# Loads of v and of three weight slices issued from GpSimd's queue, in a fused attention and SwiGLU kernel

## The chip, the core and the metric

The kernel runs on one core of a Trainium2 chip. The metric is the device time of one execution in microseconds. Times of several runs are given as a median; one execution more was taken with the hardware profiler, and all rows below come from that one.

The names in the rows: PE is TensorE's matmul, PEld its weight load, DVE is VectorE, ACT is ScalarE, POOL is GpSimd and SP is SyncE, which does no arithmetic and here issues DMA transfers. SPq and ACTq are the instructions of an engine's sequencer, DMA issues above all.

## What is computed

```python
def _attn_ref(q, k, v):                       # 4 batches, 12 heads, 448 rows, 64 columns
    scores = np.matmul(q, k.transpose(0, 1, 3, 2)) / np.sqrt(64) - np.log(448)
    attn = 1.0 / (1.0 + np.exp(-scores))
    return np.matmul(attn, v)

def _moe_ref(x, w_gate, w_val, w_out, rms_g): # x is 1792 x 768, the inner width is 1536
    rms = np.sqrt(np.mean(x * x, axis=-1, keepdims=True) + 1e-06)
    xn = x / rms * rms_g
    g = xn @ w_gate
    return g * (1.0 / (1.0 + np.exp(-g))) * (xn @ w_val) @ w_out
```

All inputs and the output are float32. The attention's weights are a sigmoid, so no row sum is needed.

## The kernel before

**Stages.** The attention goes over 24 pairs of heads (4 batches by 6). Then the SwiGLU products go over 12 slices (`fc`) of the inner width, and at the end the output products are made. The middle and the last stage begin after the attention's last pair, but the first three weight slices that the middle stage needs are loaded and prepared while the attention runs.

**One pair of the attention.** `load_qk` brings q and k of the pair, 224 KB each. On DVE `qk_hi` (L200) and `qk_lo` (L204) split them into two float16 parts in `nat_b`. `transpose` (L207) is a DMA that turns both round into `t_b`, of which there are three, so a pair's buffer is free when the pair three before it has been used by its scores. `k_swap` (L214, L215) makes two more copies of k on DVE. `scores` (L232) has 28 matmuls in four groups; ACT makes the sigmoid of each group (L234). `av` (L245) multiplies by v in 8 float32 matmuls, which the trace lists as 16. `load_v` (L195) brings v of a pair in two transfers of 128 KB into one of three buffers `v_b`.

**Order.** The order is written out by hand. The loop takes two groups of scores and then the `av` of the two groups before. Behind the four groups of pair `i` stand, in `FILL`: the transpose of pair `i + 2`; `k_swap(i + 1)` and `load_qk(i + 5)`; `qk_hi(i + 3)` and `load_v(i + 2)`; and `qk_lo(i + 3)`. Each engine and each queue works through its own list in order, and an instruction that waits for a semaphore holds everything behind it.

**Weights.** `load_w(fc, kind)` puts three transfers of 256 KB into the list `loads`; `run_load` takes one off the list after each half pair. They land in the two buffers `raw_w` (gate and val), one of each. `split_w` turns the words round on DVE (`to_f32`, L349, L352 and L353) and makes sums and float16 parts of them (L395, L398, L401). The loads of the next slice may overwrite `raw_w` only after L353 has read the buffer. The pieces of `split_w` and of the row norm (`norm`, with L275, L296 and L302) stand in the list `later`, from which the loop of the attention takes some in each step.

**SP's queue.** Before the change all loads and the DMA transposes stand in SP's one list, in program order:

```python
nc.sync.dma_start(dst, src[:, :, MID * n * D : (MID * n + 4) * D])      # v, L195
nc.sync.dma_start_transpose(out=..., in_=nat_b[i % 2]...)               # L207
nc.sync.dma_start(dst, src.rearrange("(c p) f -> p c f", p=P))          # weights, L364
```

Of the kernel before, what the change touches and what calls it, by code (L numbers as in the profile page):

```python
# [24 lines left out]
def attention_then_swiglu(  # L25
# [21 lines left out]
    nc = tc.nc  # L47
    B, H, S, D = q.shape
    DFF, DM = w_out.shape
    P = 128  # L50
    NPAIR = H // 2
    NSLOT = 2 * S // P
    MID = S // P
# [135 lines left out]
    def load_v(i):  # L189
        b, hp = pairs[i]  # L190
        t = v_b[i % 3].rearrange("p (j n) d -> p j n d", j=2)
        src = v[b, 2 * hp : 2 * hp + 2].rearrange("j (r c) d -> r j (c d)", c=NSLOT)
        for n in range(2):
            dst = t[64 * n : 64 * n + 64, :, 1 - n : 5 - n].rearrange("p j n d -> p j (n d)")
            nc.sync.dma_start(dst, src[:, :, MID * n * D : (MID * n + 4) * D])  # L195

# [159 lines left out]
    def load_w(fc, kind):  # L358


        def part(c):
            src = (w_gate, w_val)[kind][c * P : (c + 2) * P, 2 * fc * P : 2 * fc * P + 2 * P]
            dst = raw_w[kind][:, c : c + 2].rearrange("p c f w -> p c (f w)")
            nc.sync.dma_start(dst, src.rearrange("(c p) f -> p c f", p=P))  # L364

        loads.extend((fc, lambda c=c: part(c)) for c in range(0, NCC, 2))

# [307 lines left out]
    def ahead_by(n, part):  # L675
# [3 lines left out]
        (ahead_by(2, transpose),),  # L679
        (ahead_by(1, k_swap), ahead_by(5, load_qk)),  # L680
        (ahead_by(3, qk_hi), ahead_by(2, load_v)),
        (ahead_by(3, qk_lo),),
    )
# [7 lines left out]
    with tc.manual_schedule():  # L691
# [9 lines left out]
        transpose(0)  # L701
        load_qk(2)
        load_v(0)
        for part in (qk_hi, qk_lo, transpose, load_v, ahead_by(2, load_qk)):
            part(1)
# [147 lines left out]
```

## Time and profile before

| what | value |
|---|---|
| median of 3 runs | 619.05 us (617.21 to 619.07) |
| the profiled execution | 621.39 us, its span 619.6 us |
| PE busy | 599.4 us, 97% of the span |
| DVE busy | 484.4 us, 78% |
| ACT busy | 260.1 us, 42% |
| POOL busy | 1.1 us, 9 instructions |
| DMA | 62.73 MB in 84219 packets, nearly all on one queue |

Busy shares are means over stages with different limits. The attention reaches from the start to about 178 us, the SwiGLU products from there to 463 us, the output products from there to the end. A view by windows gives busy times, the granted TensorE clock (a share of 2.4 GHz: 1.00 is 2.4 and 0.50 is 1.2 GHz), the mean share of time in which the 16 DMA engines have a packet under way, and what they move.

### The profile page before, as it was taken

To read this page: it belongs to the slowest core of one execution; us is meant where nothing else is said; L and a number is where in the kernel's file an instruction comes from. 1 tells how busy PE (TensorE), PEld (TensorE's weight loads), DVE (VectorE), ACT (ScalarE), POOL (GpSimd) and SP (SyncE) were. 2 spreads that over 40 slices of the span, in tenths; PEclk is the share of its full clock that TensorE was granted. 3 is DMA by queue.
4 is the path that set the end of the run, shared out by engine and by line. 5 is a ranking of instruction groups with operands and counts; after the bars stand their busy time and mean duration, and the time that the engine had idled before them with its cause. 6 is when DMAs were issued, how large, how long until landed. Compare 5 with 4: busy or idle time off the path is not lost.

```text
span 619.6 us, 9157 instructions
## 1 busy us (share of the span) xinstructions
PE 599.4 (97%) x3594; PEld 322.9 (52%) x3594; DVE 484.4 (78%) x752; ACT 260.1 (42%) x392; POOL 1.1 (0%) x9
## 2 busy tenths in 40 slices
PE   8987999799999999999999999999999999999997
PEld 6433455364445555555555555555556666656664
DVE  4549799699879678878878878888889997776651
ACT  3666688497754423233143243243232244221020
POOL 0000000000000000000000000000000000000000
PEclk9998999799999999999999999999999999999999
DMA  7999979967500003303203113123147005121112
GB/s 176 234 242 232 251 173 228 238 157 175 142 0 2 2 0 103 100 3 103 79 24 103 53 50 103 40 63 103 58 138 314 0 7 119 30 51 26 33 46 51
DMA packets 84219, 62.73 MB, mean 101 GB/s; under 512 B 48336, under 2 KB 82640, under 8 KB 84176
## 3 DMA queue, kind: packets, MB, share of 16 engines
q1 hardware_dynamic: 83856, 61.76, 38.4%
q8 instruction: 28, 0.46, 0.3%
q10 hardware_dynamic: 320, 0.39, 0.2%
q14 instruction: 15, 0.12, 0.1%
HBM read 45.62 MB, written 5.51 MB: 83 GB/s over the span
## 4 chain that ended last, share of the span: by engine, by line
PE 84%; DMA 6%; DVE 4%; ACT 3%; issue 2%; SPq 1%; DVEq 0%; ACTq 0%
PE cc L425 13%; PE cd L425 13%; PE ca L425 13%; PE o L514 11%; PE cb L425 7%; PE av L245 6%; PE sc L232 6%; PE oc L601 4%; PE od L601 4%; PE oa L601 4%; DMA xc<-xc 4%; PE ob L601 2%; DMA xc<-in_k_dram 1%; ACT room L234 1%; PE rinv L302 1%
## 5 line engine op out<-in xcount | busy, mean ns | idle before, releaser
L425 PEld LDWEIGHTS <-wr 128*128 128x128 f16 x1512 | 147.9, 98 | 138.7 <-issue 1.2
L234 ACT ACTIVATE room<-sc,bias_s 128x896 f32<-128x896 f32 x96 | 83.9, 932 | 37.2 <-PE sc L232 37.0
L425 PE MATMUL ca<-xc,wr 128*128 128x448 f16 x432 | 89.6, 352 | 0.0
L232 PE MATMUL sc<-xc 128*64 128x448 f16 x672 | 75.9, 358 | 10.5 <-DVE xc L215 6.4
L245 PE MATMUL av<-room 128*64 128x448 f32 x384 | 84.4, 557 | 0.1
L232 PEld LDWEIGHTS <-xc 128*64 128x64 f16 x672 | 41.8, 111 | 53.6 <-issue 21.6
L425 PE MATMUL cc<-xc,wr 128*128 128x448 f16 x324 | 67.2, 352 | 0.0
L425 PE MATMUL cd<-xc,wr 128*128 128x448 f16 x324 | 67.2, 352 | 0.0
L514 PE MATMUL o<-xc,room 128*128 128x384 f16 x354 | 58.3, 326 | 0.0
L453 ACT ACTIVATE room<-ca 128x448 f32<-128x448 f32 x24 | 13.0, 543 | 90.3 <-PE ca L425 90.3
L514 PEld LDWEIGHTS <-room 128*128 128x128 f16 x354 | 34.6, 98 | 22.9
L245 PEld LDWEIGHTS av<-room 128*64 128x64 f32 x384 | 29.2, 140 | 30.1 <-issue 24.4
L425 PE MATMUL cb<-xc,wr 128*128 128x448 f16 x216 | 44.8, 352 | 0.0
L401 DVE SCALAR_TENSOR_TENSOR wr<-wr 128x768 f16<-128x768 f32 (+1 forms) x48 | 39.0, 851 | 0.1
L480 ACT ACTIVATE room<-room 128x448 f32<-128x448 f32 x24 | 13.8, 576 | 53.0 <-DVE room L479 53.0
L398 ACT ACTIVATE wr<-wr 128x768 f16<-128x768 f32 (+1 forms) x48 | 34.1, 753 | 3.5 <-DVE wr L395 3.5
L448 DVE TENSOR_TENSOR room<-room,cb 128x448 f32<-128x448 f32 x24 | 14.9, 621 | 19.6 <-PE cb L425 19.4
L353 DVE SCALAR_TENSOR_TENSOR wr<-wr 128x768 uint32<-128x768 uint32 x28 | 26.8, 957 | 0.9
L352 DVE SCALAR_TENSOR_TENSOR wr<-wr 128x768 uint32<-128x768 uint32 x28 | 26.8, 956 | 0.5
L204 DVE SCALAR_TENSOR_TENSOR xc<-xc 128x896 f16<-128x896 f32 (+1 forms) x25 | 26.3, 1051 | 0.5
L441 ACT ACTIVATE room<-ca 128x448 f32<-128x448 f32 x24 | 13.0, 544 | 32.0 <-PE ca L425 27.6
L395 DVE TENSOR_TENSOR wr<-wr 128x384 f32<-128x384 f32 x48 | 25.8, 553 | 0.8
(138 smaller groups left out, 709.4 us busy)
## 6 DMA issues: line engine op xcount, KB each, us to landing
wr<-in_moe_w_gate_dram SPq DMA_DIRECT2D x36, 256.0 KB, 3.3
wr<-in_moe_w_val_dram SPq DMA_DIRECT2D x36, 256.0 KB, 3.7
room<-in_v_dram SPq DMA_DIRECT2D x48, 128.0 KB, 3.7
xc<-in_q_dram SPq DMA_DIRECT2D x24, 224.0 KB, 3.4
xc<-in_k_dram SPq DMA_DIRECT2D x24, 224.0 KB, 3.2
out_dram<-room SPq DMA_DIRECT2D x49, 96.0 KB, 2.2
wr<-in_moe_w_out_dram SPq DMA_DIRECT2D x6, 768.0 KB, 4.3
xc<-in_moe_w_out_dram SPq DMA_DIRECT2D x5, 768.0 KB, 6.4
```

The lines of the kernel that those rows point to most:

```text
L204: stt(n[:, :, :, 1], ld_b[i % 4][:, t], SQ, n[:, :, :, 0], ALU.mult, ALU.subtract)
L232: nc.tensor.matmul(o, m, r, start=(w == 0), stop=(w == 1))
L234: nc.scalar.activation(a[:, :n], ps[:, :n, :S], AF.Sigmoid, bias=bias_s, scale=1.0 / (math.sqrt(D) * SQ * SQ))
L245: nc.tensor.matmul(ps[64 * j : 64 * j + 64, :S], v_b[i % 3][:, NG + j if g == MID else 1 + 5 * j + g], a[:, 0 if g == MID else j], start=( ...
L352: lambda: stt(b, r[:, :, 0], 29, b, ALU.logical_shift_right, ALU.bitwise_or),
L353: lambda: stt(b, r[:, :, 1], 0xC0000000, b, ALU.bitwise_and, ALU.bitwise_or),
L395: first.append((lambda o=o, f0=f0, f1=f1: tt(wf[:, o], wf[:, f0], wf[:, f1], ALU.subtract), 0.6))
L398: nc.scalar.activation(t[:, 0, s], wf[:, s], AF.Copy, scale=SW)
L401: stt(t[:, 1, s], wf[:, s], SW, t[:, 0, s], ALU.mult, ALU.subtract)
L425: nc.tensor.matmul(ps, w[:, l, b, c], xc[n, a][:, r, c], start=(not more and c == 0 and m == 0), stop=(c == NK - 1 and m == 2), skip_group ...
L514: nc.tensor.matmul(ps[:, :HALF], h[c, t // NTOK][:, l, t % NTOK * P : t % NTOK * P + P], wo[c][:, r, e * HALF : e * HALF + HALF], start=(c ...
L601: nc.tensor.matmul(ps[:, :HALF], a[x](m, l), b[y](m, r), start=(not more and m == 0 and n == 0), stop=(m == NFC // 2 - 1 and n == 2), skip ...
```

## The change

Two transfers get another issuing engine. Nothing else is changed: the same bytes go to the same places, and the program's order is the same.

```diff
@@ load_v
-            nc.sync.dma_start(dst, src[:, :, MID * n * D : (MID * n + 4) * D])
+            nc.gpsimd.dma_start(dst, src[:, :, MID * n * D : (MID * n + 4) * D])
@@ load_w, part
-            nc.sync.dma_start(dst, src.rearrange("(c p) f -> p c f", p=P))
+            queue = nc.gpsimd if fc < 3 else nc.sync
+            queue.dma_start(dst, src.rearrange("(c p) f -> p c f", p=P))
```

All 48 transfers of v and the 18 of weight slices 0 to 2 leave SP's list; slice 3 and all later ones stay. What stands behind the added line has a number higher by one (L364 is now L365).

At the start of SP's list, where the first three transposes (L207) stand between the loads of q and k (L186, L187), the difference is this:

```order
 L186 DMA xc<-in_q_dram 128x448
 L187 DMA xc<-in_k_dram 128x448
-L195 DMA room<-in_v_dram 64x2x256 x2
 L207 DMA_TRANSPOSE xc<-xc 128x14x128
-L195 DMA room<-in_v_dram 64x2x256 x2
 L186 DMA xc<-in_q_dram 128x448
 L187 DMA xc<-in_k_dram 128x448
 L186 DMA xc<-in_q_dram 128x448
 L187 DMA xc<-in_k_dram 128x448
```

The second transpose now follows the load of k directly, and the third has four transfers fewer ahead of it.

Where the loads of weight slice 2 begin, SP's list had these rows before, with the semaphores that each waits for (DVE and PE are the engines' own, DMAHW those of earlier transfers):

```order
L207 DMA_TRANSPOSE xc<-xc 128x14x128 [waits DMAHW7_49,DVE_49,PE_49]
L186 DMA xc<-in_q_dram 128x448 [waits DMAHW0_49]
L187 DMA xc<-in_k_dram 128x448 [waits DMAHW1_49]
L195 DMA room<-in_v_dram 64x2x256 [waits DMAHW2_49,PE_49]
L195 DMA room<-in_v_dram 64x2x256 [waits DMAHW3_49,PE_49]
L364 DMA wr<-in_moe_w_gate_dram 128x2x256 [waits DMAHW4_49,DVE_49]
L207 DMA_TRANSPOSE xc<-xc 128x14x128 [waits DMAHW5_49,PE_49]
```

The same transfers of v and of the weights stand in POOL's list now (DMASW are the semaphores of its own earlier transfers):

```order
L195 DMA room<-in_v_dram 64x2x256 [waits DMASW6_49,PE_49]
L195 DMA room<-in_v_dram 64x2x256 [waits DMASW7_49,DMASW5_49,PE_49]
L365 DMA wr<-in_moe_w_gate_dram 128x2x256 [waits DVE_49]
L365 DMA wr<-in_moe_w_gate_dram 128x2x256
L195 DMA room<-in_v_dram 64x2x256 [waits DMASW0_49,PE_49]
L195 DMA room<-in_v_dram 64x2x256 [waits DMASW1_49,PE_49]
```

The weight load that waits for DVE now holds the loads of v behind it, and on SP there is no such wait ahead of that transpose any more.

The start of POOL's list, behind its own memsets, is this:

```order
L195 DMA room<-in_v_dram 64x2x256 [waits Pool_49]
masks.py:199 ISA
masks.py:199 AFFINE_SELECT ident<-ident 128x128 [waits Pool_49]
L195 DMA room<-in_v_dram 64x2x256 x5
L365 DMA wr<-in_moe_w_gate_dram 128x2x256
L195 DMA room<-in_v_dram 64x2x256 [waits DMASW0_49,PE_49]
```

The v of the first three pairs and the first weights, which stood behind loads and transposes on SP, are issued with nothing of the other engines ahead of them.

## Rows read from the trace of the kernel before

**Rows 1.** Windows of core 0: stretch, its length, busy by engine (instructions), clock, DMA share, GB/s.
```profile
0.00:10.00 10.00, 8.00 (x52) 7.81 (x52) 4.44 (x9) 1.28 (x1) 1.12 (x9) 1.00 0.62 152
10.00:66.00 56.00, 48.62 (x352) 22.18 (x354) 34.20 (x64) 36.58 (x50) 0.00 (x0) 0.97 1.03 238
53.00:57.00 4.00, 4.00 (x20) 1.59 (x18) 4.00 (x7) 3.73 (x5) 0.00 (x0) 0.57 1.03 254
80.00:105.00 25.00, 24.37 (x186) 13.98 (x187) 24.42 (x37) 22.39 (x34) 0.00 (x0) 1.00 0.86 200
112.00:118.00 6.00, 6.00 (x18) 2.06 (x20) 5.88 (x7) 0.00 (x0) 0.00 (x0) 0.50 1.08 208
125.00:160.00 35.00, 33.92 (x262) 18.95 (x258) 34.25 (x51) 30.03 (x47) 0.00 (x0) 1.00 0.76 177
178.00:463.00 285.00, 285.00 (x1505) 147.21 (x1506) 238.22 (x356) 95.97 (x152) 0.00 (x0) 1.00 0.19 59
470.00:475.00 5.00, 5.00 (x33) 3.00 (x31) 4.90 (x7) 1.69 (x2) 0.00 (x0) 1.00 1.02 418
```

**Rows 2.** What PE waited for, 14 to 66 us: us in total, times, longest.
```profile
PE sc L232 <- DVE xc L215: 4.8, 5, 3.0
PE sc L232 <- DMA xc<-xc: 0.9, 3, 0.5
PE sc L232 <- ACT room L234: 0.7, 1, 0.7
```

**Rows 3.** PE in order of time: start, us, work, count, [idle before, releaser].
```profile
52.39 2.01 PE L232 MATMUL sc<-xc 128*64 128x448 f16 x14 [3.02 <-DVE xc L215]
...
111.97 1.86 PE L302 MATMUL rinv<-room,ones 112*128 112x448 f32 x2 [2.72 <-DVE room L296]
```

**Rows 4.** SP's queue in order of time: start, us, issue, count.
```profile
10.64 2.17 SPq L207 DMA_TRANSPOSE xc<-xc  x1
12.90 1.38 SPq L195 DMA_DIRECT2D room<-in_v_dram  x2
...
16.92 3.67 SPq L207 DMA_TRANSPOSE xc<-xc  x1
...
43.08 0.59 SPq L364 DMA_DIRECT2D wr<-in_moe_w_val_dram  x1
...
85.50 1.32 SPq L195 DMA_DIRECT2D room<-in_v_dram  x2
90.46 0.38 SPq L364 DMA_DIRECT2D wr<-in_moe_w_gate_dram  x1
90.94 2.64 SPq L207 DMA_TRANSPOSE xc<-xc  x1
...
98.36 2.75 SPq L207 DMA_TRANSPOSE xc<-xc  x1
...
104.86 3.11 SPq L207 DMA_TRANSPOSE xc<-xc  x1
```

**Rows 5.** What SP's queue waited for, 86 to 92 us.
```profile
SPq L364 <- DVE wr L353: 3.6, 1, 3.6
```

**Rows 6.** DVE in order of time, as in rows 3.
```profile
47.50 0.56 DVE L349 TENSOR_SCALAR wr<-wr 128x768 uint32<-128x768 uint32 x1 [2.32 <-DMA wr<-in_moe_w_val_dram]
...
51.94 0.39 DVE L215 COPY xc<-xc 64x896 f16<-64x896 f16 x1
...
110.27 0.39 DVE L214 COPY xc<-xc 64x896 f16<-64x896 f16 x1 [1.48 <-DMA xc<-xc]
...
111.08 0.84 DVE L296 TENSOR_SCALAR room<-ident,y 112x112 f32<-112x112 f32 x4
```

**Rows 7.** Issues of v, weights (to 178 us) and transposes: ns min/median/max, first and last start.
```profile
L195 SPq DMA_DIRECT2D room<-in_v_dram x48: 595/622/1296, 9.1 to 161.5; - x48
L364 SPq DMA_DIRECT2D wr<-in_moe_w_val_dram x12: 397/555/592, 36.5 to 162.2; - x12
L207 SPq DMA_TRANSPOSE xc<-xc x24: 1538/2588/3837, 5.8 to 157.4; - x24
```

## The prediction

> **What bounds the kernel now.** I read the windows first. From 178 to 463 us PE is busy for 285.00 of 285.00 us at full clock [rows 1], and the output products behind it begin when that ends. Nothing that the change touches can shorten this part: the weights of slice 3 and later keep their queue, and PE waits for none. So the change is worth what it gives or takes in the attention, the first 178 us.
>
> There PE has gaps. The reader should see three things. First, between 14 and 66 us PE waits 4.8 us in five gaps for the copies of k, 0.9 us for the transposes directly and 0.7 us for ACT, 6.4 us in all [rows 2]; 3.02 us of it is one gap that ends at 52.39 [rows 3]. Secondly, a gap of 2.72 us ends at 111.97 [rows 3]. Thirdly, behind both long gaps the granted clock is lower: 0.57 on the mean of 53 to 57 us and 0.50 (1.2 GHz) from 112 to 118 us [rows 1]. PE is busy all through both windows, so they lose 4.0 x 0.43 = 1.7 us and 6.0 x 0.50 = 3.0 us of work. The short gaps have no such echo: the 0.97 of the window from 10 to 66 us is used up by the 1.7 us.
>
> Then I followed each long gap backwards. *The first*: the copy that PE waits for (L215) starts at 51.94, and DVE had stood still for 2.32 us until 47.50, for a val weight load [rows 6] that SP issued only at 43.08 [rows 4]. *The second*: PE waits for L296 at 111.08, which stands behind the copy L214 in DVE's order; that copy began at 110.27 after 1.48 us of waiting for a transpose [rows 6], which SP issued at 104.86 [rows 4]. Why so late? After the loads of v at 85.50, which end at 86.82, SP's list stops at a weight load until 90.46 [rows 4]: the buffer is still being read by L353 on DVE, 3.6 us [rows 5]. The transpose behind that load needs nothing of it. It goes at 90.94, and the next two follow 7.4 and 6.5 us apart, at 98.36 and 104.86 [rows 4]: the lag is never made up. A short list on SP is thus held by transfers that are not urgent.
>
> **The change part by part.** *A, the stretch up to 66 us.* SP loses 0.62 us for each v transfer and 0.56 us for each weight transfer (medians of rows 7); a pair with weights has two of each, 2.4 us out of about 6.5. The third transpose, at 16.92, has four v transfers fewer ahead of it, of which the two at 12.90 alone took 1.38 us [rows 4]. If SP's order is all that is late, the 6.4 us of gaps and the 1.7 us of clock go: 8.1 us. The other end is nothing, because the DMA engines are full too: from 10 to 66 us their share is 1.03 at 238 GB/s, and a full share goes with 418 GB/s where the packets are larger [rows 1]. The bytes stay the same, so a pair can't come sooner than its bytes do. What is free is the beginning: the share is 0.62 from 0 to 10 us [rows 1], so 10 x 0.38 = 3.8 us of DMA work can be put there, and the change does so: POOL asks for six v transfers and one weight transfer at once, 1024 KB, 4.4 us at 238 GB/s. I take 3.8 us of the 8.1 us, since the row of the full DMA engines lies nearest. The price at the beginning, that these bytes run beside the first q and k, is between 0 and 4.4 us; I put it inside the 3.8 us, as it is paid out of free share.
>
> *B, the gap at 111.97.* With v and the weights gone, nothing on SP between 86.82 and 90.46 waits for L353. The transpose behind it comes up to 3.6 us earlier and the one at 104.86 by more, as its two forerunners lose four v and four weight transfers. DVE's 1.48 us go. Late next is DVE itself, which had worked without a stop until 108.79: L296 comes 1.48 us earlier and PE's gap shrinks from 2.72 to 1.24 us. Gaps of this size had no lower clock behind them (above), so the 3.0 us go too: 1.5 + 3.0 = 4.5 us. If the clock falls all the same, it is 1.5 us.
>
> *C, POOL's own work.* POOL does 1.12 us in the whole attention [rows 1], so the 66 transfers (48 of v, 18 of weights) find it free. The weight load that waited for L353 now holds v on POOL; v is issued two pairs ahead, so the same 3.6 us fits in about two times 6 us. Four transfers in a pair of 6.5 us leave 1.6 us for each before POOL's queue is itself late; SP needs at most 1.30 us for one [rows 7]. What an issue by POOL costs the others no row shows. The nearest rows say 0 for DVE, as SP's issues cost it nothing, and as the upper end one issue time, 0.62 us, in which DVE would stand still. It counts where DVE is full: 24.42 of 25 us (80 to 105) and 34.25 of 35 us (125 to 160) [rows 1]. In them lie eight pairs of v transfers (the first at 85.50) and five weight transfers, 21: 0 to 13.0 us. I take a tenth, 1.3 us, near the lower end because the list of DVE is untouched. A gain from C has no place to come from.
>
> *Sum.* 3.8 + 4.5 - 1.3 = 7.0 us. The profiled execution took 621.39 us and would take 614.4. The median of the runs is 2.34 us lower, at 619.05; the same gain gives **612.0 us**.
>
> **The rivals.** *The transfers only change hands.* The DMA engines are full before and after (1.03, [rows 1]), so A is 0; PE still idles 1.24 us at 111, the clock falls, B is 1.5, and C takes 1.3: 618.9 us, no change. For it speaks the share; against it, that at 86.82 to 90.46 SP stands still, and from 80 to 105 us the share is only 0.86. The Trainium skill ("DMA: Bandwidth & Descriptors", section "Issuing engines are not separate DMA queues") says the same in general: DMAs of all issuing engines end on the same 16 DMA engines, and issuing from several saves only sequencer time, "usually small relative to the DMA itself". By that rule A and B would be near 0; the trace agrees on the full engines, but the 3.6 us wait is sequencer time of a kind that the rule leaves out.
>
> *POOL holds up DVE.* Each POOL issue stops DVE for 0.62 us in the two full windows: 21 x 0.62 = 13.0 us against 8.3 gained, 4.7 us slower, **623.8 us**. It decides from 8.3 / 21 = 0.40 us per transfer. For it speaks that DVE has only 0.6 and 0.75 us of room in those windows; against it, that PE has 1.1 us of room in the second and that no row shows the two engines stopping each other. The Trainium skill ("SBUF — State Buffer", section "SBUF: two separate sides") has such a rule: descriptors of GpSimd's DMAs are written by its cores over a port pair that they share with VectorE, under an exclusive lock, so that the later of the two waits. It measures 3100 ns in place of 620 ns for a transfer beside a VectorE copy; an estimate from that page is 2.5 us more for v, which two pairs of lead would hide. No run shown here bears on it.
>
> *The DMA engines yield more with two queues.* Then A is the whole 8.1 us: 8.1 + 4.5 - 1.3 = 11.3, **607.8 us**, and 606.4 without C. Against it: to be 8 us shorter from 10 to 66 us they would have to move about 260 GB/s even after the 3.8 us put ahead, and the fullest window here shows 254 [rows 1].
>
> **How the numbers follow.** Forecast, 608.5 to 616.5 us: 0.50. Whole gain, below 608.5: 0.12. A small gain of 1.9 to 2.5 us: 0.03. Only change of hands: 0.13. POOL holds up DVE, from 620.9 up: 0.22. A measurement of this kernel can tell about 0.3% (1.9 us) from no change. So faster 0.65, same 0.13, slower 0.22. The range leaves out a little of the whole gain (0.05) and half of the slow case (0.11): 605 to 623.
>
> **What would show it.** SP should show no wait of L207's list for L353 before 140 us, and the transpose now at 104.86 should be issued at least 5 us earlier, counted against the pair's first scores. The gap at 52.39 and the window at 0.57 should be gone; the gap at 111.97 should be near 1.2 us with clock 1.00 behind it. The DMA share of the first 10 us should rise from 0.62 towards 1. A is wrong if PE's gaps up to 66 us stay; B, if the clock still falls around 110 us; C, if L200, L214 and L215 take longer or have idle time ahead of them while a POOL transfer is issued, or if PE's `av` begins to wait for v. A start of the first scores much later than before would show the early v transfers in the way of q and k.

## The result

| kernel | median, us | runs | ratio to before |
|---|---|---|---|
| before | 619.01 | 617.21 to 619.07 | |
| changed, first measurement | 627.82 | 623.62, 624.34, 631.30, 631.39 | 1.0145 [1.0108, 1.0182] |
| changed, a second time (e13, below) | 622.83 | 614.82, 617.94, 627.73, 630.16 | none: the four spread over 15 us |

The forecast was 612.0, range 605 to 623. In the first measurement the change makes the kernel 1.4% slower. The second doesn't repeat that size: its median is 3.6 us above the 619.27 us of the kernel before beside it, and its shortest execution is shorter than all of those. What holds over both is that one execution is unlike the next: eight of them lie between 614.8 and 631.4, with 626.0 in the middle, and six of the eight are above 623. The ratios below leave out executions that lie over 1.5% above the shortest of their kernel; where that happens the range and the median are of all of them.

(A correction to the description ahead of the prediction: the weights arrive as 64-bit floats, which is why `to_f32` converts them and why a slice is 2 x 768 KB. Nothing in the sum rests on it.)

The rows below are from the shortest execution of the first measurement, 623.62 us with a span of 621.8. From the first SwiGLU product to the end it takes 445.2 us, before 445.1, so all of the difference lies in the attention, as forecast. This execution is only 2.2 us longer than the one profiled before (621.39 us); the longer executions of this measurement were not profiled, so the rows show the ways in which time is won and lost, and not the 8.8 us between the medians. The windows answer [rows 1]:

```profile
0.00:10.00 10.00, 8.30 (x50) 8.11 (x50) 4.34 (x8) 1.28 (x1) 5.49 (x16) 1.00 0.86 200
10.00:66.00 56.00, 47.95 (x352) 25.23 (x352) 32.48 (x51) 36.76 (x50) 16.56 (x25) 0.97 1.12 225
53.00:57.00 4.00, 2.75 (x20) 1.09 (x16) 2.17 (x3) 3.63 (x6) 1.93 (x3) 1.00 0.91 218
66.00:80.00 14.00, 10.58 (x66) 4.60 (x68) 9.69 (x28) 5.72 (x8) 1.19 (x2) 0.88 0.93 214
80.00:105.00 25.00, 24.19 (x184) 13.27 (x181) 24.57 (x35) 22.65 (x35) 9.13 (x14) 1.00 0.95 202
112.00:118.00 6.00, 3.79 (x26) 1.44 (x22) 5.38 (x23) 3.77 (x6) 1.19 (x2) 1.00 1.20 277
125.00:160.00 35.00, 33.86 (x264) 19.23 (x262) 34.40 (x45) 29.95 (x47) 6.37 (x11) 1.00 0.82 178
```

The free share of the first 10 us is used in part: 0.62 became 0.86, and 152 became 200 GB/s. From 10 to 66 us the engines are busier than before (1.12 for 1.03) and move less (225 for 238 GB/s). The low clock at 53 to 57 and at 112 to 118 us is gone, but PE now idles there, and a new window at 0.88 follows at 66 us. What PE waited for from 14 to 66 us, against [rows 2]:

```profile
PE sc L232 <- DVE xc L215: 2.6, 4, 1.2
PE sc L232 <- DMA xc<-xc: 1.6, 1, 1.6
PE sc L232 <- ACT room L234: 0.4, 2, 0.2
```

Here the change does what was hoped: 4.6 us for 6.4, and the 3.02 us gap of [rows 3] is 1.2 us. The loss lies on either side of it. PE in order of time:

```profile
12.65 0.38 PE L232 MATMUL sc<-xc 128*64 128x448 f16 x2 [3.25 <-DMA xc<-xc]
...
57.59 0.38 PE L232 MATMUL sc<-xc 128*64 128x448 f16 x2 [1.63 <-DMA xc<-xc]
58.48 1.52 PE L232 MATMUL sc<-xc 128*64 128x448 f16 x14 [0.51 <-DVE xc L215]
...
67.31 0.38 PE L232 MATMUL sc<-xc 128*64 128x448 f16 x2 [2.06 <-DMA xc<-xc]
68.20 2.82 PE L232 MATMUL sc<-xc 128*64 128x448 f16 x14 [0.51 <-DVE xc L215]
...
116.87 1.02 PE L302 MATMUL rinv<-room,ones 112*128 112x448 f32 x2 [2.21 <-DVE room L296]
```

Three of these waits are for a transpose (xc<-xc by DMA). The same fourteen matmuls take 1.52 us at 58.48 and 2.82 us at 68.20: the clock fell behind the gap. Where the pairs begin (first score matmul of pair 0, 6, 8, 10, 13, 16, and the first SwiGLU product, all read from PE's list in time):

| kernel | p0 | p6 | p8 | p10 | p13 | p16 | SwiGLU |
|---|---|---|---|---|---|---|---|
| before | 9.9 | 49.0 | 66.2 | 80.4 | 97.8 | 123.7 | 174.5 |
| after, 623.62 | 12.6 | 48.4 | 67.3 | 84.1 | 101.5 | 125.6 | 176.6 |
| after, 614.82 (e13) | 12.5 | 47.9 | 61.0 | 75.5 | 92.9 | 116.8 | 167.7 |

The start loses 2.7 us, the way to pair 6 wins 3.3, the stretch to pair 10 loses 4.3, and pairs 13 to 16 win 1.8. The cause of the middle loss stands in the transposes. All 24 of them, before and then after, issue to landing:

```profile
DMA to landing us min/median/max: 4.0/4.8/6.1
```
```profile
L207 SPq DMA_TRANSPOSE xc<-xc x24: 1510/2262/5663, 5.8 to 158.8; - x24
...
  DVE xc L214: 23.7, 8
...
DMA to landing us min/median/max: 4.0/6.6/14.2
```

The median went from 4.8 to 6.6 us and the longest from 6.1 to 14.2; DVE's first copy of k (L214) waits 23.7 us for them (16.9 before). While the worst ones are under way, GpSimd's list reads:

```profile
35.26 0.73 POOL L365 DMA_DIRECT2D wr<-in_moe_w_val_dram  x1
44.12 0.92 POOL L365 DMA_DIRECT2D wr<-in_moe_w_gate_dram  x1 [8.14 <-DVE wr L353]
45.03 1.22 POOL L195 DMA_DIRECT2D room<-in_v_dram  x2
46.23 1.47 POOL L365 DMA_DIRECT2D wr<-in_moe_w_gate_dram  x2
47.67 1.23 POOL L195 DMA_DIRECT2D room<-in_v_dram  x2
48.87 1.49 POOL L365 DMA_DIRECT2D wr<-in_moe_w_val_dram  x2
```

The list stands for 8.14 us for L353, with v behind the weight load, and then nine transfers, 5 x 256 + 4 x 128 = 1792 KB, go out in 6.2 us: 294 GB/s asked of engines that had moved 238. SP's transposes fall into that:

```profile
46.45 3.11 SPq L207 DMA_TRANSPOSE xc<-xc  x1
...
53.03 5.44 SPq L207 DMA_TRANSPOSE xc<-xc  x1
...
62.02 5.56 SPq L207 DMA_TRANSPOSE xc<-xc  x1
```

By the packet records of the trace they land after 7.8, 13.7 and 9.8 us, and 544, 528 and 240 KB of GpSimd's packets are served between their first packet and their last. A transpose that has the engines to itself moves its 448 KB in 2.3 us.

Sharing during a transpose's own packets is the smaller part of the lateness, though. Summed over the 24 transposes, the packet records show 66.2 us from first packet to last before and 78.5 after, but 37.3 us from issue to first packet before and 61.0 after. Two thirds of the added time pass before the first packet, mostly behind the loads of q and k on SP's own list: the transpose issued at 36.9 us has its first packet at 43.2, when the load of q issued at 34.4 has landed (43.1). These loads land later as well (medians; before, then after):

```profile
xc<-in_q_dram SPq DMA_DIRECT2D x24, 224.0 KB, 3.4
xc<-in_k_dram SPq DMA_DIRECT2D x24, 224.0 KB, 3.2
```
```profile
xc<-in_q_dram SPq DMA_DIRECT2D x24, 224.0 KB, 5.5
xc<-in_k_dram SPq DMA_DIRECT2D x24, 224.0 KB, 5.0
```

In the five kernels with v on GpSimd and all transposes they take 4.6 to 5.5 us, and 3.0 and 3.4 us in the same kernel with only the first three transposes (e10 below). So SP's whole list falls behind, and it takes both the second queue and the transposes.

The costs of issue, against [rows 7]:

```profile
L195 POOL DMA_DIRECT2D room<-in_v_dram x48: 598/602/868, 1.4 to 160.7; - x48
...
  PE av L245: 102.2, 17
```
```profile
L365 POOL DMA_DIRECT2D wr<-in_moe_w_gate_dram x9: 728/736/917, 5.4 to 97.2; - x9
...
  DVE wr L353: 14.5, 3
```

GpSimd needs 0.60 us for 128 KB and 0.74 us for 256 KB, where SP needed 0.62 and 0.56. On DVE the three lines that could show a hold-up, after and then before, in the first 178 us (busy, mean ns of one, idle):

```profile
L200 DVE TENSOR_SCALAR xc<-xc 128x896 f16<-128x896 f32 x23 | 14.7, 638 | 3.1 <-DMA xc<-in_k_dram 3.0
...
L214 DVE COPY xc<-xc 64x896 f16<-64x896 f16 x24 | 9.6, 402 | 26.0 <-DMA xc<-xc 23.7 <-PE av L245 1.9
L215 DVE COPY xc<-xc 64x896 f16<-64x896 f16 x24 | 9.5, 396 | 0.3
```
```profile
L200 DVE TENSOR_SCALAR xc<-xc 128x896 f16<-128x896 f32 x23 | 14.3, 621 | 3.9 <-DMA xc<-in_k_dram 3.8
...
L215 DVE COPY xc<-xc 64x896 f16<-64x896 f16 x24 | 9.3, 389 | 0.3
L214 DVE COPY xc<-xc 64x896 f16<-64x896 f16 x24 | 9.3, 387 | 20.0 <-DMA xc<-xc 16.9 <-PE sc L232 2.5 <-PE ssq L275 0.2
```

Together 0.4 + 0.3 + 0.2 = 0.9 us, for 66 transfers. The second profile of the changed kernel (e13) has 637, 402 and 394 ns for them, and e15 below, in which GpSimd issues nothing after the first 10 us, 622, 387 and 390.

### The profile page after: what moved, and what is told of

Read it like the earlier page. It is cut to its first block, busy times and chain, and to the rows that moved or that the text cites. A ratio compares the mean times of both kernels' runs of the same rounds, so it can differ in the third digit from the quotient of the medians.

```text
span 621.8 us, 9168 instructions
## 1 busy us (share of the span) xinstructions
PE 597.7 (96%) x3594; PEld 325.6 (52%) x3594; DVE 485.0 (78%) x752; ACT 260.2 (42%) x392; POOL 43.6 (7%) x75
## 4 chain that ended last, share of the span: by engine, by line
PE 80%; DVE 8%; DMA 7%; issue 2%; ACT 2%; DVEq 0%; ACTq 0%
PE cd L426 13%; PE cc L426 13%; PE ca L426 13%; PE o L515 11%; DMA xc<-xc 7%; PE cb L426 7%; PE sc L232 4%; PE av L245 4%; PE oc L602 4%; PE od L602 4%; PE oa L602 4%; PE ob L602 2%; DVE xc L204 1%; ACT room L234 1%; DVE xc L200 1%
## 5 line engine op out<-in xcount | busy, mean ns | idle before, releaser
L232 PE MATMUL sc<-xc 128*64 128x448 f16 x672 | 77.8, 364 | 14.2 <-DMA xc<-xc 7.7
L245 PE MATMUL av<-room 128*64 128x448 f32 x384 | 81.9, 541 | 0.0
L232 PEld LDWEIGHTS <-xc 128*64 128x64 f16 x672 | 44.0, 112 | 55.6 <-issue 22.3
L454 ACT ACTIVATE room<-ca 128x448 f32<-128x448 f32 x24 | 13.1, 544 | 90.3 <-PE ca L426 90.3
L515 PEld LDWEIGHTS <-room 128*128 128x128 f16 x354 | 34.6, 98 | 22.9
L195 POOL DMA_DIRECT2D room<-in_v_dram x48 | 29.4, 617 | 102.2 <-PE av L245 102.2
L214 DVE COPY xc<-xc 64x896 f16<-64x896 f16 x24 | 9.6, 402 | 26.0 <-DMA xc<-xc 23.7
L353 DVE SCALAR_TENSOR_TENSOR wr<-wr 128x768 uint32<-128x768 uint32 x28 | 26.8, 957 | 0.9
```

What stands on the lines that cost most here:

```text
L195: nc.gpsimd.dma_start(dst, src[:, :, MID * n * D : (MID * n + 4) * D])
L232: nc.tensor.matmul(o, m, r, start=(w == 0), stop=(w == 1))
L245: nc.tensor.matmul(ps[64 * j : 64 * j + 64, :S], v_b[i % 3][:, NG + j if g == MID else 1 + 5 * j + g], a[:, 0 if g == MID else j], start=( ...
L353: lambda: stt(b, r[:, :, 1], 0xC0000000, b, ALU.bitwise_and, ALU.bitwise_or),
L515: nc.tensor.matmul(ps[:, :HALF], h[c, t // NTOK][:, l, t % NTOK * P : t % NTOK * P + P], wo[c][:, r, e * HALF : e * HALF + HALF], start=(c ...
```

## The experiments

The theory after the result: a transpose that shares the engines with a second queue lands late, whoever issues it. On SP's one list it follows what stands ahead of it and meets only that and what stands behind it. The rivals: the crowded start alone; GpSimd holding DVE up; large packets of the second queue taking the turns of the transpose's small ones (the packet records show 256 B for a transpose, 1024 B for v and weights on SP's or ACT's queue, 4096 B on GpSimd's). Edits are against the kernel before unless another is named; the time before was 619.1 to 619.7 us beside all of them.

**One part alone: v (e1), the three slices (e2).**

```diff
 # e1, load_v                      # e2, part(c)
-nc.sync.dma_start(...)            -nc.sync.dma_start(...)
+nc.gpsimd.dma_start(...)          +(nc.gpsimd if fc < 3 else nc.sync).dma_start(...)
```

> Only v goes to POOL's queue, the weights stay on SP. Theory P (POOL's transfers travel in 4096 B packets, a transpose in 256 B packets, and the DMA engines alternate between queues by packet, so a transpose starves while POOL has bytes under way): v is 128 KB at a time, so a transpose meets at most 256 KB; transposes land in 4 to 6 us where in the changed kernel 6.6 us was the median and 14.2 the worst; the start still loses about 2 us since v of three pairs is asked for at once. Time 615 to 621 us. Theory Q (any second queue beside the transposes costs, whatever its packets): the 48 transfers of v are the larger number, so most of the loss stays, 623 to 627 us. Theory S (POOL's issues hold up DVE): 48 of 66 issues stay, so about 0.7 of the loss, 625 us.

> Only weight slices 0 to 2 go to POOL's queue, v stays on SP. Theory P: the weights are 256 KB each and three to four stand in POOL's queue together, so the transposes in the stretches with weights still land late (8 us and more): 621 to 628 us. Theory Q: only 18 transfers are left beside the transposes, so a third of the loss: 620 to 623 us. Theory S: 18 of 66 issues, 621 us. SP's wait for L353 at 87 us is gone in all of them.

Measured: v alone 619.24 us (612.41 to 625.29, ten runs), ratio 0.9973 [0.9944, 1.0002]; the weights alone 616.80 (613.96 to 621.51), 0.9970 [0.9937, 1.0003]. Neither does harm; together they cost 8.8 us in the first measurement and 3.6 in the second. Theory P's time for v came true, its landings of 4 to 6 us did not; for the weights all three theories named times above what was measured. In e1 the transposes land late too (median 6.2, longest 10.4 us), and what SP's shorter list gains seems to pay for it; the runs already scatter over 13 us. In e2 all of slice 0 goes out in the first 10 us, its first scores are at 12.8, and pair 8 begins at 62.3 in place of 66.2.

**The crowded start (e4).** The changed kernel with the first transfers back on SP:

```diff
-nc.gpsimd.dma_start(dst, src[:, :, MID * n * D : (MID * n + 4) * D])
+(nc.gpsimd if i >= 3 else nc.sync).dma_start(dst, src[...])
-queue = nc.gpsimd if fc < 3 else nc.sync
+queue = nc.gpsimd if fc < 3 and (fc, kind, c) != (0, 0, 0) else nc.sync
```

> As the changed kernel, but v of the first three pairs and the first weight transfer stay on SP, so nothing of POOL's runs beside the first loads. The first scores should begin at 9.9 us as before and not at 12.65. If the crowded start is the main cause, the whole loss goes: 612 to 620 us. If the transposes starve later (theory P), 2 to 3 us come back: about 625 us.

Measured: 631.39 us (629.40 to 634.53), 1.0188 [1.0137, 1.0238]. The first scores are at 9.9 us again, and it is the slowest of all, above both times that were named: what had gone in the first 10 us now goes beside later transposes, which land after up to 13.9 us. The start is a loss of its own, but not the cause.

**Another issuer and other packets (e3, e6, e5, e11).** The weights of the first three slices on ACT's queue: e3 as they are, e6 in halves, e5 and e11 as one transfer of 768 KB for each kind.

```diff
-nc.sync.dma_start(dst, src.rearrange("(c p) f -> p c f", p=P))
+# e3, 1024 B: (nc.scalar if fc < 3 else nc.sync).dma_start(dst, ...)
+# e6, 512 B:  for a in range(2): nc.scalar.dma_start(d4[:, a], s4[:, a])
+# e5, 6144 B: if c == 0: nc.scalar.dma_start(whole, rows of 6 * 2 * P words)
+# e11, 1024 B: if c == 0: nc.scalar.dma_start(whole, every.rearrange("(c p) f -> p c f", p=P))
```

> Weight slices 0 to 2 are issued by ACT in place of SP, v stays on SP: a second queue, as in the run with the weights on POOL, but its packets are 1024 B as on SP. Theory P: a packet is a quarter as long, so the transposes keep more of the engines and land in 5 to 7 us in the stretches with weights; ACT pays 18 issues of about 0.5 us, and its sigmoids wait behind the loads that wait for L353. The time is below the run with the weights on POOL by 2 us or more. Theory Q: the same landing times as with the weights on POOL, and the time is no better than that run.

> Weight slices 0 to 2 on ACT's queue as in e3_w_act, in packets of 512 B and six transfers in place of three. Theory P: the transposes keep a larger share and land in 5 to 6 us. Theory M: the same bytes take longer in smaller packets, so they stand beside the transposes longer; landing 7 us or more in the stretches with weights. ACT issues 18 more transfers of about 0.5 us, which alone may cost 2 to 4 us.

> Weight slices 0 to 2 on ACT's queue as in e3_w_act, but each kind as one transfer of 768 KB in rows of 6144 B (it brings other columns of the weights, so the output is another one). The packets are six times as long. Theory P (a long packet of the second queue takes an engine's turn from the 256 B packets of a transpose): transposes that meet them land in 9 us or more, against 6.8 to 7.6 us at worst in e3_w_act, and the time is 3 us or more above e3_w_act. Theory M (a transpose runs far below its speed as long as any packets of another queue stand between its own, and the 16 engines wait for one another): what counts is how long both are under way, not the size; landing times as in e3_w_act or shorter, as the bytes go faster in long packets; time within 3 us of e3_w_act.

> The first three weight slices go out on ACT's queue, one transfer of 768 KB for each kind, all six blocks at once, in rows of 1024 B; everything else is as before. It is the same burst as in the kernel with rows of 6144 B (transposes landed after up to 13.3 us, 627.6 us), with packets a sixth as large. If the packets' size decides (an engine that takes turns between two queues gives a 256 B packet of a transpose a turn for each large one), transposes that meet the loads land after at most 8 us, and the time is 618 to 622 us. If the size of the burst decides, or the mere mixing, they land after 11 to 14 us and the time is 625 to 629 us.

| kernel | packets, one transfer | longest landing, us | median (range), us | ratio |
|---|---|---|---|---|
| e6 | 512 B, 128 KB | 7.6 | 625.74 (625.70 to 625.77) | 1.0110 [1.0081, 1.0139] |
| e3 | 1024 B, 256 KB | 8.2 | 620.34 (617.86 to 624.25) | 1.0010 [0.9989, 1.0032] |
| e11 | 1024 B, 768 KB | 11.3 | 622.13 (619.85 to 625.78) | 1.0051 [1.0023, 1.0078] |
| e5 | 6144 B, 768 KB | 14.0 | 627.58 (626.07 to 629.09) | 1.0140 [1.0100, 1.0180] |

e5 and e6 have two executions each. GpSimd isn't needed for late landings. With the packets held at 1024 B the larger burst goes with 11.3 in place of 8.2 us (e3, e11); with the burst held at 768 KB the larger packets go with 14.0 (e11, e5). The medians of the time stand in the same order. That speaks for both, but each landing is the longest of one execution, and two executions of the changed kernel differ by as much (14.2 and 10.0, e13 below). Theory P got both its numbers for e5, but not its time for e3, which was to be below e2's 616.80. The two theories of e11 each got one number: the time that packets foretold (618 to 622; 622.13 lies at its edge), the landing that the burst foretold (11 to 14). In the time ACT's own work has a part: over the attention PE waits 8.6, 5.8 and 5.1 us for ACT's sigmoids in e3, e11 and e5, and 2.2 us before. What PE waits for from 14 to 66 us in e11, then in e5:

```profile
PE sc L232 <- DMA xc<-xc: 5.2, 1, 5.2
```
```profile
PE sc L232 <- DMA xc<-xc: 9.2, 2, 8.0
```

e6 is slow for another reason and decides little: ACT issues twice as many transfers, and in its attention PE waits 16.1 us for ACT's sigmoids.

**Some slices (e8, e7, e12).** Slice 2 alone on GpSimd is step B by itself; then slices 1 and 2; then all three, with slice 0 held back until the loop reaches the place where SP would have begun to load it.

```diff
+queue = nc.gpsimd if fc == 2 else nc.sync            # e8
+queue = nc.gpsimd if fc in (1, 2) else nc.sync       # e7
+queue = nc.gpsimd if fc < 3 else nc.sync             # e12, and ahead of load_w(0, 0):
+nc.vector.memset(raw_w[0][:, 0:1, 0:1, 0:1].bitcast(F32), 0.0)
```

> Only weight slice 2 goes to POOL. This is term B of the prediction by itself: SP no longer stands still for L353 at 87 us. By the prediction 4.5 us are gained in the gap near 110 us, 614 to 615 us. If the transposes that meet the six transfers land late enough to keep the gap (theory M with full weight), 618 to 620 us. The stretch up to 66 us should be as before, with its gap of 3 us and low clock.

> Only weight slices 1 and 2 go to POOL, slice 0 and v stay on SP. In e2_w_pool the whole of slice 0 was asked for in the first 10 us, the first transpose landed after 6.3 us and the clock was low from 11.4 to 18.3 us. With slice 0 back on SP the start is as before (first scores at 9.9 us, clock 1.00). Theory M: 12 transfers are left to meet the transposes, SP does not wait for L353 at 87 us, so the gap of 2.7 us near 110 us and its low clock go: 611 to 615 us, faster than before and than e2_w_pool. If the loss comes from POOL's issues as such, 618 us.

> The weights of the first three slices on GpSimd's queue, v on the sync engine (616.8 us against 619.7 in that form before), and the first of these loads held back by one word that VectorE writes into its buffer where the kernel before begins to load the weights, so that slice 0 no longer travels beside the first q and k. If the late first scores (12.8 for 9.9 us) and the low clock from 11.4 to 18.3 us of that form come from the early loads, they go, the first scores stand at 10 us again and the time is 611 to 615 us. If the gain of that form came just from having slice 0 done in the first ten us, before the transposes begin in earnest, the loads now meet the second to fourth transposes, these land after 8 to 14 us, and the time is 619 to 627 us.

Measured: e8 619.39 us (616.73 to 621.29), 0.9999 [0.9979, 1.0019]: the second of its two numbers, and a miss for step B. SP's wait of [rows 5] is gone, and in the profiled execution pairs 13 to 16 take 22.9 us in place of 25.9, but the gap stays and only the low clock behind it goes:

```profile
111.83 1.02 PE L302 MATMUL rinv<-room,ones 112*128 112x448 f32 x2 [2.02 <-DVE room L296]
```

The two matmuls of L302 take 1.02 us here and 1.86 in [rows 3]. The medians show none of the 3.0 us; the transpose that meets the loads lands after 9.0 us. e7, a miss of both its numbers: 622.65 (619.32 to 627.21), 1.0058 [1.0026, 1.0091]; its longest landing is 17.9 us, beside the loads of slice 1. e12: 625.58 (620.63 to 630.24), 1.0094 [1.0059, 1.0129]. Its first scores are back at 10.0 us, and six transfers, 1536 KB, go out from 21.0 to 25.5 into the fourth transpose, which lands after 11.5 us by the packet records. That is the second of its two numbers: what e2 gained it gained by having slice 0 done before the transposes come close upon each other.

**The transposes taken away (e9, e10).** The direct test: both kernels with only the first three transposes. The other 21 are left out, so the later pairs compute on old tiles and the output is another one.

```diff
 def transpose(i):
+    if i >= 3:
+        return
```

> The kernel before with only the first three transposes; the later pairs compute on the tiles that these left, so the transposes of pairs 3 to 23 are left out with their DMA work. It is the base for the run of the changed kernel with the same cut. 20 transposes of 2.3 us active time are gone: 606 to 614 us, PE with no gap for the copies of k behind a transpose between 30 and 130 us.

> The changed kernel with only the first three transposes; those of pairs 3 to 23 are left out. If the transposes are the victims of the second queue, the change can no longer do harm beyond the start: between 5 us faster and 3 us slower than the kernel before with the same cut (the later start of the first scores, 2.7 us, stays in both theories). If GpSimd's transfers hurt through something else (DVE held up, the engines simply losing rate, v coming late), the changed kernel stays 6 to 11 us slower than that base, as the whole kernels do (8.8 us).

Measured: 608.35 us (608.06 to 608.64) before, 611.28 (611.12 to 611.42) after: 2.9 us apart in place of 8.8. The start is as late as in the whole kernels, as their first scores and the wait for the first transpose show (before, then after):

```profile
9.91 0.38 PE L234 MATMUL sc<-xc 128*64 128x448 f16 x2 [0.91 <-DMA xc<-xc]
```
```profile
12.84 0.58 PE L235 MATMUL sc<-xc 128*64 128x448 f16 x2 [4.37 <-DMA xc<-xc]
```

12.84 - 9.91 = 2.9 us. Of these 1.9 are left at pair 8 and 2.4 at the first SwiGLU product of the profiled executions, so GpSimd's 66 transfers do little other harm where there is no transpose to meet. The scatter is gone with the transposes: 0.3 us where the whole changed kernel has 17. Two thirds of the 8.8 us, net of what SP's shorter list gains, go by way of the transposes. What the test can't tell apart: it takes away the transposes' bytes, and the path from the loads of q and k to the scores, together with the transposes.

**The scatter (e13, e14).** The changed kernel once more; and the changed kernel with slices 1 and 2 back on SP, so that GpSimd's list never waits for DVE.

```diff
 # e14, against the changed kernel
-queue = nc.gpsimd if fc < 3 else nc.sync
+queue = nc.gpsimd if fc == 0 else nc.sync
```

> The changed kernel itself once more, beside the next two on the same chip. Its spread should be as in the first measurement, 623 to 632 us with a median of 625 to 629. Without the transposes of pairs 3 to 23 its executions lay within 0.3 us of each other, so the longer executions should differ from the shortest by transposes that land late and, behind them, by stretches at the lower clock, and by nothing before the first scores (12.6 us) or after the attention.

> The changed kernel with the weights of slices 1 and 2 back on the sync engine: v and slice 0 stay on GpSimd. GpSimd's list then never waits for VectorE, and no burst of nine transfers goes out around 44 us. If that burst is the cause, the time is 613 to 620 us (the gain of slice 0 in the first 10 us, and v alone, which cost nothing). If the sum of what lies on the second queue is the cause, little is won: 623 to 628 us.

Measured: e13 614.82 to 630.16 us, median 622.83, below what was expected. e14 621.19 in the median (611.21 to 628.05, ten runs). Neither theory on e14 holds: three executions are as fast as the burst theory asked (611.2 to 613.0), four lie at 620 to 623, three from 623.6 up. (The three alone are at 0.9881 [0.9864, 0.9898] of the kernel before.) The profiles make the scatter readable in part, as they caught the shortest execution of e13 and a longer one of e14 (623.62). GpSimd's lists are the same up to 36 us, shifted by 0.9 us; e13, then e14:

```profile
28.78 1.21 POOL L195 DMA_DIRECT2D room<-in_v_dram  x2 [3.02 <-PE av L245]
29.97 1.46 POOL L365 DMA_DIRECT2D wr<-in_moe_w_val_dram  x2
```
```profile
29.68 1.21 POOL L195 DMA_DIRECT2D room<-in_v_dram  x2 [3.02 <-PE av L245]
30.88 1.46 POOL L365 DMA_DIRECT2D wr<-in_moe_w_val_dram  x2
```

The transposes behind them, issued at 24.0, 31.6 and 37.3 us in e13, land after 6.5, 5.3 and 5.7; those of e14, issued at 25.0, 32.5 and 42.1, after 10.1, 16.5 and 11.1. In the first profile of the changed kernel, the one issued at 31.3 took 9.0. Amid the one issued at 32.5 us in e14 1008 KB of GpSimd's packets were served, amid the one issued at 31.6 in e13 none. The landings in e13 and its window from 10 to 66 us, and then what PE waited for from 14 to 66 us in e14:

```profile
DMA to landing us min/median/max: 4.0/5.3/10.0
```
```profile
10.00:66.00 56.00, 51.61 (x376) 24.68 (x378) 38.67 (x74) 38.62 (x52) 16.69 (x25) 0.94 1.12 262
```
```profile
PE sc L232 <- DMA xc<-xc: 6.1, 1, 6.1
```

PE waits for no transpose there in e13. The clock adds to it, and perhaps more than the waits do: in the 623.62 us execution of the first measurement the attention has 6.8 us at 1.2 GHz and the mean granted clock is 0.994; the executions above 631 us have 0.981 and 0.983. By an estimate from these numbers, span times (1 - clock), the lower clock takes at most (with PE busy all through) 3.7 us of the first and 12.0 us of the longest (631.39), which is 8.3 us more where the times differ by 7.8. In e14 it is 1.8 to 11.9 us where the times differ by 16.8. The profiles show the low clock behind gaps of PE; which gaps the longest executions had, no trace shows. So the burst behind the 8.1 us wait in the first profile was one way into the same trouble, not the cause: in e14 GpSimd has no wait for DVE, and it scatters alike.

**Slice 0 alone (e15), and when it should go (e17, e16).**

```diff
+queue = nc.gpsimd if fc == 0 else nc.sync                          # e15
+nc.vector.memset(raw_w[0][:, 0:1, 0:1, 0:1].bitcast(F32), 0.0)     # e17: e15, ahead of transpose(0)
+nc.vector.memset(raw_w[0][:, 0:1, 0:1, 0:1].bitcast(F32), 0.0)     # e16: e15, behind k_swap(0)
```

> The kernel before with the weights of slice 0 alone on GpSimd; they go out in the first 10 us. If what the weights of three slices gained on GpSimd (616.8 against 619.7) comes from slice 0, and slices 1 and 2 took some of it back (they alone gave 622.7 against 619.5), this gives 611 to 615 us. If moving slice 0 is worth no more than the late first scores cost (2.9 us and 3.4 us of lower clock), it gives 618 to 621 us.

> Slice 0 of the weights alone on GpSimd (615.05 us without a gate), its first load held back until VectorE has split the first q and k, at about 6 us. If the first scores came late because these bytes travelled beside the first q and k, the first scores are at 10 to 11 us and the time is 611 to 614 us. If it was the first transpose (issued at 5.9) that the bytes stretched, the loads meet it all the same: first scores at 12 to 14 us, 614 to 617 us.

> The same with the word written behind VectorE's copies of the first k, at about 10.7 us, so that the first pair meets none of these bytes: first scores at 10 us. The loads, 1536 KB in some 5 us, then meet the second transpose, issued at about 10.8. If a transpose that meets a burst lands late, its landing goes from 4 to 7 us or more, the second pair's scores start 3 to 6 us late, and the time is 613 to 619 us; if only the first q and k were the victims, 611 to 613 us.

Measured: e15 **615.05 us** (614.98 to 615.43), 0.9931 [0.9913, 0.9949]: faster than both kernels, and its runs agree within 0.5 us. e17 618.60 (616.44 to 622.54), 1.0013 [0.9990, 1.0037]; e16 617.66 (616.65 to 620.01), 0.9989 [0.9970, 1.0008]. In e15 the six loads are issued from 1.36 to 6.12 us, and the windows show them in the free share of the start:

```profile
0.00:10.00 10.00, 8.29 (x50) 8.10 (x50) 4.34 (x8) 1.28 (x1) 5.50 (x15) 1.00 0.82 251
10.00:66.00 56.00, 50.23 (x372) 24.90 (x374) 36.89 (x72) 38.61 (x52) 0.00 (x0) 0.97 1.06 235
```
```profile
DMA to landing us min/median/max: 4.0/4.9/6.9
```

251 GB/s for 152, and no transpose lands later than 6.9 us. The price is the first scores at 12.9 us and 3.4 us of low clock behind them; at pair 8 the kernel is 5.0 us ahead all the same (61.2 for 66.2). Of the two numbers named for e15 the first came true, at its edge. Holding the loads back to save that price costs more than the price: in e16 the first scores are at 9.9, but the loads, issued from 11.04 to 15.48, meet the second and third transposes (8.4 us at the longest) and pair 2 begins at 27.6 in place of 25.1. In e17, from 6.23 to 10.66, the first scores are at 11.5, the second transpose lands after 9.2 us by the packet records, and PE waits 2.5 us for v: its time lies above both that were named. e16 is as its first theory had it.

## Why the prediction was wrong

**The step that failed** is A's two ends, "SP's order is all that is late" and "the DMA engines are full too". Both count bytes and issues only. The working shortened SP's list and let each transpose come earlier by what was taken from ahead of it; no term asked what a transpose, and the loads of q and k around it, meet once they are issued, so their landing time was kept as it had been without a reason. The runs show it at 6.6 in place of 4.8 us in the median and up to 14.2. A list in order had two effects, delay and shelter, and only the delay was priced. With the transposes taken away the loss falls from 8.8 to 2.9 us (e9, e10), so the missing term is some 6 us by the medians of the first measurement, net of what the shorter list gained. The forecast counted 7.0 us of gain, and 627.82 us lies 15.8 us above it. In single executions the distance from the forecast runs from 2.8 us (614.82) to 19.4 (631.39).

**A, by its own sizes.** The 3.8 us of free share at the start were there: slice 0 alone, put into it, gains 619.27 - 615.05 = 4.2 us (e15), net of the price. The changed kernel used half of it: 200 - 152 = 48 GB/s more over the first 10 us are 480 KB, 2.0 us at 238 GB/s, since q and k lost part of what v and the first weights took. The price was taken as "inside the 3.8", from bounds of 0 to 4.4 us. The first scores are late by 2.7 us, as the last of the signs of being wrong had it, and by 2.9 us in e10 against e9, on top. All later transfers of v and of the weights go out beside the transposes.

**B.** SP's wait for L353 goes, as said, and the low clock at 112 us goes. The 4.5 us don't come: the profile of e8 shows 3.0 of them between pairs 13 and 16, its median 0.1 (interval from 1.3 us of gain to 1.2 of loss). The gap itself was to shrink from 2.72 to 1.24 us; it is 2.21 in the changed kernel and 2.02 in e8. The wait for a transpose didn't go, it moved one pair ahead: in e8 DVE waits for the one that lands after 9.0 us beside the loads of slice 2, and works without a stop from there to L296.

```profile
104.81 0.39 DVE L214 COPY xc<-xc 64x896 f16<-64x896 f16 x1 [1.53 <-DMA xc<-xc]
```

**C** was near in size by luck: its tenth of 13.0 us was a guess, 1.3 us, for two windows; 0.9 us were found on DVE over the whole attention, as slightly longer instructions and not as standing still.

**The rivals.** "POOL holds up DVE" gave 623.8 us, and the profiled execution took 623.62. That nearness is chance: DVE lost 0.9 us, not 13.0, and in e11 and e5 transposes land after up to 11.3 and 14.0 us without GpSimd. Of the rule of the Trainium skill that the prediction named beside it ("SBUF — State Buffer", section "SBUF: two separate sides"), by which GpSimd's descriptor writing and some of VectorE's instructions lock each other out of a port pair that they share, these 0.9 us are the most that a run here shows. "The DMA engines yield more with two queues" asked for about 260 GB/s from 10 to 66 us; the shortest execution, e13's, has 262 there, the first profile 225. "The transfers only change hands" (618.9 us) came out in the number for v alone and for slice 2 alone (619.24 and 619.39 us). The Trainium skill says beside it that transfers of different issuers run on the same 16 engines "and interleave with each other" ("DMA: Bandwidth & Descriptors", section "Issuing engines are not separate DMA queues"); the packet records agree. The prediction read that sentence for the bandwidth and passed over the word that mattered here.

**What stays open**: what decides, at nearly the same issue times, whether a transpose finishes ahead of the second queue's packets or in their midst (5.3 or 16.5 us). Which part of the scatter is the lower clock's and which the waits' stays open too. The packet records show stretches, such as 62 to 66 us in the first profile, in which some 20 packets are under way on the 16 engines and little is moved (20 to 76 GB/s). The size of the packets and of the burst may both move it (e3, e11, e5); no run here separates the engines' way of taking turns from the transposes' own traffic.

## What to carry to other kernels

Before moving transfers off a busy queue, list what the remaining urgent ones will meet: a queue in order is also a shelter, and a short list on SP is worth little if a burst from elsewhere shares the engines with its transposes. Move what can be done entirely in a stretch with free DMA share and hardly a transpose (slice 0 in the first 10 us, beside the first one: 4.2 us gained and a scatter of 0.5 us), and leave beside the urgent transfers what must travel with them. Look at the spread of the runs as well as the median; a profile is one execution, and here the one profiled may be 16 us from another.

## What the hardware showed that was not expected

- A transpose of 448 KB that has the engines to itself is active for 2.3 us. With a second queue's packets among its own it took 2.2 to 6.6 us for 207 to 270 KB of them (all kernels), 7.0 us for 531 KB (e11), 7.2 us for 704 KB (e12), 12.0 us for 768 KB in packets of 6144 B (e5) and 10.9 us for 1008 KB (e14). In the first profile alone it took 5.4 us for 544 KB and 9.0 us for 528. More bytes go with more time, and leave a factor of two or three open.
- Rows of 1024 B travel as packets of 4096 B on GpSimd's queue and of 1024 B on SP's and ACT's.
- Kernels in which no later transpose met a second queue agree within 0.3 to 0.6 us from run to run (e9, e10, e15, four executions each); with v on a second queue the spread is 13 to 17 us (e1, e14 and the eight executions of the changed kernel) and 5 us in e4. The kernel before, which has one queue and all transposes, still spreads over 3 to 6 us; why, no run here shows.
